# Two small multiplies per pass go from VectorE to GpSimd in a gated mix of two attentions

## The chip, the core and the metric

The kernel runs on one core of a Trainium2 chip. A core has five engines with their own instruction queues: TensorE (PE in the profile; PEld is its weight load), VectorE (DVE), ScalarE (ACT), GpSimd (POOL) and SyncE (SP), which here only issues DMAs. Each engine works through its queue in order, and the queues meet only at semaphores. The metric is the device time of one execution in microseconds; lower is better.

## The reference

The input x (2048 tokens, 512 wide) goes through two attention blocks of 32 heads of width 16, and a gate per token mixes the results:

```python
g = sigmoid((x * gate_w).sum(-1, keepdims=True))
a = A_ref(x, A_wq, A_wk, A_wv, A_wo, A_beta)
b = B_ref(x, B_wqkv, B_wo)
return g * a + (1 - g) * b
```

Block B is plain softmax attention over all 2048 keys. Block A cuts the tokens into four segments of 512, with causal softmax attention inside a segment and a linear memory M, z of the segments before it:

```python
p = softmax(q @ k.T * scale + mask); a_dot = p @ v
a_mem = (phi(q) @ M) / (phi(q) @ z + 1e-6)
o = sigmoid(beta) * a_mem + (1 - sigmoid(beta)) * a_dot
```

Both outputs go through an output projection. So for each head and token the kernel needs the softmax numerator, a denominator, and a factor for the numerator: g (1 - sigmoid(beta)) / denominator for A, (1 - g) / denominator for B.

## The kernel before, in words

The attention is cut into 64 units: 32 of A (u = 0 to 31) and 32 of B (u = 32 to 63). A unit is one group of four heads (qd) in one segment of 512 queries (c). The order of all instructions is written out by hand. After a first stage of projections, the main loop runs over k = 0 to 31; here one turn of it is called pass k. Pass k does B's unit 32 + k and A's unit k.

A pass is a sequence of steps n. In each of the first 32 steps PE computes a group of scores (`t_group`, L537) into PSUM, ACT turns an earlier group into exponentials (L543), and PE multiplies exponentials by V (`pv`, L559) into the bank pvb; V carries a column of ones, so row 16 of each head's result is the denominator. Woven between the matmuls of the step is one task of a *later* unit: `s_b` (L474) computes scores once more, two matmuls into one half of a double buffer (sbk), and DVE takes their row maximum with a reduce (L476), so that the exponentials can be shifted by it. There is one such reduce in each of the 32 steps, up to pass 30. Five more steps do A's unit: scores, exponentials, a triangular mask on POOL (`affine_select`, L546), and A's row maxima (`s_a`).

What the change touches is the end of a unit, spread over the next pass. `fin_copy` copies pvb out of PSUM and stores it (pd). `fin_load` loads back the numerators (o) and the denominators (rec, 128 partitions x 16). `fin_rec` (L580 on) takes the reciprocal on DVE, multiplies it by the gate, and stores it (rd, L589). `fin_bc` (L595) loads rd spread over the rows of a head (d), and `fin_norm` (L599, L604) multiplies numerators by d on POOL. In pass k the call `beside(k, it)` (it is half of n) runs `fin_rec` for B's unit 31 + k at it = 5 and for A's unit k - 1 at it = 6. `fin_norm` for two units at a time follows in the even passes, at it = 9 for B and 13 for A. `m_chain`, which prepares the row maxima of the next units, stands at it = 10; from pass 7 on it runs on POOL behind one small DVE reduce (L485, then L494 to L497). `m_rows` (it = 12) transposes its result on PE, and SP writes it into the q tiles (L515).

The gate columns were prepared long before: grow[:, 0] holds g, grow[:, 1] holds 1 - g, and nq holds 1 - sigmoid(beta), one column for each qd.

Of the kernel before, what the change touches and what calls it, by code (L numbers as in the profile page):

```python
# [12 lines left out]
OP = mybir.AluOpType  # L13
# [21 lines left out]
def gated_mix_kernel(ctx, tc, xt, wq, wk, wv, wo, beta, wqkv, wob, gate_w, out):  # L35
    nc = tc.nc
# [18 lines left out]
    grow = P.tile([128, 2, NC4, E], FT, name="grow")  # L55
    gh = P.tile([128, 4], FT, name="gh")
    nh = P.tile([128, 4], FT, name="nh")
    nq = P.tile([128, 8], FT, name="nq")
# [521 lines left out]
    def fin_rec(u):  # L580
        kd, qd, c = UN[u]
        r = AT.pop(("r", u))
        nc.vector.reciprocal(r, r)
        if kd == "A":
            nc.vector.scalar_tensor_tensor(r, r, nq[:, qd:qd + 1], grow[:, 0, c], op0=OP.mult, op1=OP.mult)
        else:
            nc.vector.tensor_tensor(r, r, grow[:, 1, c], op=OP.mult)
        AT["rd", u] = D.tile([128, E], FT, name=f"rd{u}")
        nc.sync.dma_start(AT["rd", u], r)  # L589

# [146 lines left out]
    early = st33[:EARLY]  # L737
# [21 lines left out]
    for blk in range(16):  # L759
        g, c = divmod(blk, 4)  # L760
# [135 lines left out]
    def beside(k, it):  # L896

        for f, it0, u in ((fin_load, NT + 1, 32 + k), (fin_rec, 5, 31 + k), (fin_bc, 6, 31 + k),
                          (fin_load, 1, k - 1), (fin_rec, 6, k - 1), (fin_bc, S_LAST + 2, k - 1)):
            if it == it0 and (k or it0 > NT):  # L900
                f(u)
        c, j = divmod(k - 1, 8)
        if k and j % 2:
            for kd, it0 in (("B", 9), ("A", 13)):
                if it == it0:
                    fin_norm(kd, j // 2, c)
        if k >= 8 and k % 2 == 0 and it == NT + 2:
            out_split(k // 8 - 1, k // 2 % 4)
        if (k, it) == (31, 4):
            grest = AT["grest"] = AT["o"][0][64:, 0, 0]  # L910
            nc.sync.dma_start(grest, GD[3 * C:].rearrange("(o t) -> o t", o=1).to_broadcast([64, C]))
        if (k, it) == (31, 9):
            grest = AT["grest"]
            nc.vector.tensor_scalar(grest, grest, nh[64:, 3:4], None, op0=OP.mult)
        if (k, it) == (31, NT + 2):
            fin_rec(63)
        if k == 31 and it == 13:
            o = AT["o"][1][:64, 3, 0]
            nc.gpsimd.tensor_tensor(o, o, AT["d"][0][:64], op=OP.mult)
        if k == 31 and it < 8 and it % 2 == 0:  # L920
            for a in range(2):
                tail_split(it // 2, slice(0, 3), a)
# [109 lines left out]
```

## Time and profile before

| | |
|---|---|
| median of 3 runs | 1946.82 us |
| lowest and highest | 1943.4 and 2188.65 us |
| profiled execution | 1946.74 us |
| its span in the trace | 1945.0 us |
| granted TensorE clock, mean | 0.997 |
| fin_rec's instructions on DVE | 63 reciprocals (L583), 31 for A (L585), 32 for B (L587) |

The span is the time from the first to the last instruction that the profiler recorded; 1.74 us of the profiled execution lie outside of it. In the rows of the profile a line such as `1000.17 0.24 DVE L583 RECIPROCAL rec<-rec` reads: start in us from the span's start, time in us, engine, line of the kernel, operation, output and input; `x8` at the end means that eight like instructions were merged into one row. A bracket tells how long the engine had been idle and what it had waited for.

### The profile page before, as it was taken

The numbers are of one execution on the slowest core, as the hardware profiler recorded it, in microseconds if no ns is written. First come the engines' busy times: TensorE is split into PE (matmuls) and PEld (weight loads), VectorE is DVE, ScalarE is ACT, GpSimd is POOL, SyncE is SP. The second block draws the span as 40 slices with busy tenths as digits, with TensorE's granted clock in tenths as the row PEclk, the third lists the DMA queues.
The fourth block names the chain that finished last, engine by engine and source line by source line (L and its number), as shares of the span: only waits on it lengthen the run. The fifth ranks groups of instructions, "written<-read, shape, count | busy, mean of one in ns | idle before, by whom it ended". The sixth has DMA issues, their size and how long they took to land.

```text
span 1945.0 us, 43560 instructions
## 1 busy us (share of the span) xinstructions
PE 1922.5 (99%) x17485; PEld 931.0 (48%) x17485; DVE 1622.1 (83%) x1726; ACT 1434.8 (74%) x2699; POOL 298.4 (15%) x593
## 2 busy tenths in 40 slices
PE   7999999999999999999999999999999999999999
PEld 5887777444344444444444444444444444444445
DVE  6135766899999999999999999999999999999942
ACT  4233333688888888888888888888888888888884
POOL 5200000011111111111111111111111111111022
PEclk9999999999999999999999999999999999999999
DMA  7666656745444444443445454544444443434111
GB/s 217 163 207 185 196 193 173 176 96 116 98 117 88 105 87 105 87 116 87 116 87 114 87 115 87 116 88 108 94 97 107 96 105 87 104 87 110 50 48 58
DMA packets 163790, 222.49 MB, mean 114 GB/s; under 512 B 39916, under 2 KB 90556, under 8 KB 157828
## 3 DMA queue, kind: packets, MB, share of 16 engines
q1 hardware_dynamic: 159284, 211.41, 44.1%
q0 software_dynamic: 3248, 8.03, 2.3%
q8 instruction: 138, 2.26, 0.5%
q14 instruction: 64, 0.52, 0.1%
q10 hardware_dynamic: 1056, 0.26, 0.1%
HBM read 147.95 MB, written 68.16 MB: 111 GB/s over the span
## 4 chain that ended last, share of the span: by engine, by line
PE 96%; DVE 2%; DMA 1%; SPq 1%; issue 0%; ACT 0%; DVEq 0%; ACTq 0%
PE pvb L559 33%; PE tb L537 18%; PE sbk L474 12%; PE mb L537 9%; PE tb L304 5%; PE sbk L452 3%; PE tb L625 2%; PE mb L304 2%; PE sbk L287 1%; PE tb L287 1%; PE mb L625 1%; PE pvb L304 1%; PE sbk L456 1%; PE mb L287 1%; PE pvb L287 1%; PE tb L652 1%
## 5 line engine op out<-in xcount | busy, mean ns | idle before, releaser
L476 DVE TENSOR_REDUCE mxb<-sbk 128x2 f32<-128x1024 f32 x1024 | 1225.8, 1223 | 61.0 <-PE tb L537 30.6
L543 ACT ACTIVATE raw<-tb 128x512 f32<-128x512 f32 x1555 | 887.6, 598 | 148.2 <-PE tb L537 103.6
L559 PE MATMUL pvb<-raw,vb 128*17 128x256 f32 (+1 forms) x8072 | 639.9, 388 | 0.0
L543 ACT ACTIVATE raw<-mb 128x512 f32<-128x512 f32 x782 | 467.6, 598 | 72.3 <-PE mb L537 45.7
L474 PE MATMUL sbk<-xh,qb 64*128 64x512 f32 x1344 | 477.6, 444 | 3.5 <-DVE mxb L476 2.1
L537 PE MATMUL tb<-qb,xh 64*128 64x512 f32 x872 | 353.3, 443 | 0.0
L559 PEld LDWEIGHTS pvb<-raw,vb 128*17 128x17 f32 x8072 | 135.0, 95 | 341.3 <-issue 335.9
L474 PE MATMUL sbk<-kb,qb 64*128 64x512 f32 x704 | 240.9, 444 | 0.0
L537 PEld LDWEIGHTS tb<-qb,xh 64*128 64x128 f32 x872 | 146.4, 184 | 176.6 <-issue 90.1
L537 PE MATMUL mb<-qb,xh 64*128 64x512 f32 x445 | 199.0, 447 | 0.0
L474 PEld LDWEIGHTS sbk<-xh,qb 64*128 64x128 f32 x1344 | 190.6, 184 | 8.7 <-DVE mxb L476 6.3
L537 PE MATMUL tb<-qb,kb 64*128 64x512 f32 x470 | 191.0, 446 | 0.9 <-DVE st L314 0.9
L546 POOL TENSOR_SCALAR_AFFINE_SELECT raw<-raw 128x256 f32<-128x256 f32 (+1 forms) x320 | 115.6, 361 | 357.7 <-ACT raw L543 349.9
L460 DVE TENSOR_REDUCE mx<-sbk 128x2 f32<-128x768 f32 (+1 forms) x128 | 136.7, 1090 | 23.7 <-PE sbk L456 20.9
L537 PEld LDWEIGHTS mb<-qb,xh 64*128 64x128 f32 x445 | 82.0, 184 | 94.9 <-issue 50.6
L537 PEld LDWEIGHTS tb<-qb,kb 64*128 64x128 f32 x470 | 79.2, 184 | 99.0 <-issue 53.1
L599 POOL TENSOR_TENSOR o<-o,d 128x512 f32<-128x512 f32 x31 | 39.7, 1280 | 477.7 <-DMA d<-rd 388.5
L537 PE MATMUL mb<-qb,kb 64*128 64x512 f32 x234 | 104.1, 445 | 0.0
L474 PEld LDWEIGHTS sbk<-kb,qb 64*128 64x128 f32 x704 | 96.1, 184 | 5.2 <-issue 3.4
L559 PE MATMUL pvb<-raw,va 128*17 128x256 f32 (+2 forms) x1280 | 94.7, 384 | 0.8 <-ACT pvs L568 0.8
L452 PE MATMUL sbk<-ka,qa 64*128 64x256 f32 (+3 forms) x512 | 88.0, 358 | 1.1
L311 ACT ACTIVATE st<-tb 128x512 fp32r<-128x512 f32 x33 | 19.8, 599 | 81.1 <-DVE phi L310 46.8
(288 smaller groups left out, 1864.3 us busy)
## 6 DMA issues: line engine op xcount, KB each, us to landing
xh<-dB SPq DMA_DIRECT2D x38, 512.0 KB
vb<-vdB SPq DMA_DIRECT2D x16, 1088.0 KB
dB<-st SPq DMA_DIRECT2D x64, 256.0 KB
dA<-st SPq DMA_DIRECT2D x64, 256.0 KB
pd<-pvs SPq DMA_DIRECT2D x64, 256.0 KB
kb<-dB SPq DMA_DIRECT2D x22, 512.0 KB
xh<-dB SPq DMA_DIRECT2D x38, 256.0 KB
qb<-dB SPq DMA_DIRECT2D x64, 128.0 KB
```

The costliest lines, as they stand in the source:

```text
L287: nc.tensor.matmul(b, lhs, WV[wi][:, k, :], start=n == 0, stop=n == 11)
L304: nc.tensor.matmul(b, WS[ws][w][wi][:, k, :], (XH, XL)[xi][c][:, k, :], start=n == 0, stop=n == 11)
L452: nc.tensor.matmul(b[:, j, c0:c0 + n], q_of(u)[r, p, i * 128:(i + 1) * 128], k_of(u, p)[r, :n], start=True, stop=False)
L460: nc.vector.tensor_reduce(m[:, :, p, i], b[:, :, :n], axis=AX.X, op=OP.max)
L474: nc.tensor.matmul(b[:, j], q_of(u)[r, p, i * 128:(i + 1) * 128], k_of(u, p)[r, kc * C:(kc + 1) * C], start=True, stop=True)
L476: nc.vector.tensor_reduce(MXB[u][:, :, p, i, kc], b, axis=AX.X, op=OP.max)
L537: nc.tensor.matmul(bs[j][:, c0:c0 + w], k_of(u, h // 2)[r, 128 * it:128 * it + 128], q_of(u)[r, h // 2, q0:], start=True, stop=True)
L543: nc.scalar.activation(pt, bs[j], AF.Exp, scale=SCALE)
L546: nc.gpsimd.affine_select(out=m, in_=m, pattern=[[1, 128]] if n < 2 else [[0, 2], [1, 128]], compare_op=OP.is_ge, fill=0.0, base=0, channe ...
L559: nc.tensor.matmul(PVB[32 * h:32 * h + E + 1, q0 + lo:q0 + hi], vt[:, it, 4 * q + h, :], pt[:, lo:hi], start=it == 0 and lo == 0, stop=it ...
L599: nc.gpsimd.tensor_tensor(o, o, d, op=OP.mult)
L625: nc.tensor.matmul(b, (AT["oh"], AT["ol"])[oi][:, g, a], (AT["wh"], AT["wl"])[wi][:, g, a], start=n == 0, stop=n == 11)
```

## The change

`early` is true for A's units 0 to 6 and 31 and for B's units 32 to 38 and 63. Those keep their form. For all others the multiply by the gate is issued on GpSimd. For A, one DVE instruction with two multiplications (by the column of nq, then by grow) becomes two POOL instructions; for B, one becomes one. Since the units 7 to 30 and 39 to 62 are finished in the passes 8 to 31, it is these 24 passes that change. The reciprocal stays on DVE, and the store of rd stays on SP.

```diff
         r = AT.pop(("r", u))
         nc.vector.reciprocal(r, r)
-        if kd == "A":
+        early = u % 32 < 7 or u in (31, 63)
+        if kd == "A" and not early:
+            nc.gpsimd.tensor_scalar(r, r, nq[:, qd:qd + 1], None, op0=OP.mult)
+            nc.gpsimd.tensor_tensor(r, r, grow[:, 0, c], op=OP.mult)
+        elif kd == "A":
             nc.vector.scalar_tensor_tensor(r, r, nq[:, qd:qd + 1], grow[:, 0, c], op0=OP.mult, op1=OP.mult)
         else:
-            nc.vector.tensor_tensor(r, r, grow[:, 1, c], op=OP.mult)
+            (nc.vector if early else nc.gpsimd).tensor_tensor(r, r, grow[:, 1, c], op=OP.mult)
         AT["rd", u] = D.tile([128, E], FT, name=f"rd{u}")
         nc.sync.dma_start(AT["rd", u], r)
```

On VectorE, in the first half of a pass, the queue before reads (rec is the tile with the 128 x 16 denominators, mxb the row maxima, sbk_114 and sbk_115 the two halves of the double buffer):

```order
L476 TENSOR_REDUCE mxb<-sbk_115 128x2
L583 RECIPROCAL rec<-rec 128x16
L587 TENSOR_TENSOR rec<-rec,grow 128x16
L476 TENSOR_REDUCE mxb<-sbk_114 128x2
L476 TENSOR_REDUCE mxb<-sbk_115 128x2
L583 RECIPROCAL rec<-rec 128x16
L585 SCALAR_TENSOR_TENSOR rec<-rec,nq,grow 128x16
L476 TENSOR_REDUCE mxb<-sbk_114 128x2
```

and at the same place of the changed kernel:

```order
L476 TENSOR_REDUCE mxb<-sbk_115 128x2
L583 RECIPROCAL rec<-rec 128x16
L476 TENSOR_REDUCE mxb<-sbk_114 128x2
L476 TENSOR_REDUCE mxb<-sbk_115 128x2
L583 RECIPROCAL rec<-rec 128x16
L476 TENSOR_REDUCE mxb<-sbk_114 128x2
```

The two multiplies are gone; the reduces and reciprocals keep their order.

On GpSimd, the changed kernel's queue from the masks of one pass to those of the next reads as follows (the new rows are L591 for B and L586 and L587 for A; L603 is the line that was L599 before the change; the brackets name the semaphores that an instruction waits for):

```order
L546 AFFINE_SELECT raw_86<-raw_86 128x2x128 [waits Activation_49] x6
L591 TENSOR_TENSOR rec<-rec,grow 128x16 [waits DMAHW4_49,DVE_49]
L586 TENSOR_SCALAR rec<-rec,nq 128x16 [waits DMAHW6_49,DVE_49]
L587 TENSOR_TENSOR rec<-rec,grow 128x16 [waits Pool_49]
L603 TENSOR_TENSOR o_2775<-o_2775,d_2779 128x512 [waits DMAHW7_49,DMAHW6_49,DMAHW5_49]
L494 TENSOR_SCALAR mx<-mx 128x32 [waits DVE_49]
L495 CAST mhi<-mx 128x32 [waits Pool_49]
```

The three new instructions stand between the masks and `fin_norm`; what came before stays in its order.

On SyncE, the stores of the gates in the first half of a pass read before

```order
L589 DMA rd_13448<-rec 128x16 [waits DMAHW4_49,DVE_49]
L595 DMA d_2779<-rd_13448 64x1x512 [waits DMAHW5_49,DMAHW4_49]
L589 DMA rd_13475<-rec 128x16 [waits DMAHW6_49,DVE_49]
L394 DMA qa_74<-dA_118 32x2x512 [waits DMAHW7_49,PE_49]
L394 DMA qa_74<-dA_118 32x2x512 [waits PE_49]
```

and now

```order
L593 DMA rd_13460<-rec 128x16 [waits DMAHW4_49,Pool_49]
L599 DMA d_2779<-rd_13460 64x1x512 [waits DMAHW5_49,DMAHW4_49]
L593 DMA rd_13488<-rec 128x16 [waits DMAHW6_49,Pool_49]
L394 DMA qa_74<-dA_118 32x2x512 [waits DMAHW7_49,PE_49]
L394 DMA qa_74<-dA_118 32x2x512 [waits PE_49]
```

Only the wait differs: the stores wait for POOL where they waited for DVE.

## The prediction

> **What bounds the kernel now.** I read the page first, then the stages, then the chain that ended last, and last the rows around one place that the change touches. The page's first part and its chain:
>
> ```profile
> PE 1922.5 (99%) x17485; PEld 931.0 (48%) x17485; DVE 1622.1 (83%) x1726; ACT 1434.8 (74%) x2699; POOL 298.4 (15%) x593
> PE 96%; DVE 2%; DMA 1%; SPq 1%; issue 0%; ACT 0%; DVEq 0%; ACTq 0%
> ```
>
> TensorE (PE) is the bound: it is never free for long, and the chain runs along it. That doesn't yet say that the other engines cost nothing, because a matmul that waits for a PSUM bank hides inside a busy neighbour. A stretch from the middle shows how near VectorE (DVE) stands to it (columns: stretch, length, then busy time and instructions of PE, weight loads, DVE, ACT, POOL, then granted clock, DMA share, GB/s):
>
> ```profile
> core 0: us, PE busy (x) PEld busy (x) DVE busy (x) ACT busy (x) POOL busy (x), PEclk, DMA share, GB/s
> 1000.00:1200.00 200.00, 199.86 (x2036) 84.09 (x2036) 186.12 (x182) 167.08 (x311) 30.58 (x64) 1.00 0.44 99
> ```
>
> There DVE is busy 186 of 200 us, at a granted clock of 1.00, and POOL 31. So PE sets the pace with DVE close behind, and a DVE instruction costs time only where it makes a PSUM bank come free too late. Such places can be seen in the rhythm of the chain. One step of a pass ends in eight rows of the PV product (L559), and a step's length is the distance between two of these (three excerpts of the chain: pass 9, pass 13, pass 30):
>
> ```profile
> 804.41 0.56 PE pvb L559 x8
> 805.62 0.56 PE pvb L559 x8
> 807.00 0.56 PE pvb L559 x8
> ...
> 1002.65 0.56 PE pvb L559 x8
> 1003.86 0.56 PE pvb L559 x8
> 1005.24 0.56 PE pvb L559 x8
> ...
> 1846.56 0.56 PE pvb L559 x8
> 1847.92 0.56 PE pvb L559 x8
> ```
>
> A step takes 1.21 to 1.22 us (804.41 to 805.62, 1002.65 to 1003.86). One step takes 1.38, 1.38 and 1.36 in these three passes: 0.16, 0.16 and 0.14 us too long. Here is why, at the middle one:
>
> ```profile
> 1003.14 0.18 PEld L537 LDWEIGHTS tb<-qb,xh 64*128 64x128 f32 x1 [0.42 <-issue]
> 1003.14 0.29 PEld L474 LDWEIGHTS sbk<-xh,qb 64*128 64x128 f32 x2
> 1003.24 4.61 DVE L476 TENSOR_REDUCE mxb<-sbk 128x2 f32<-128x1024 f32 x4
> 1004.36 0.18 PEld L537 LDWEIGHTS tb<-qb,xh 64*128 64x128 f32 x1 [0.42 <-ACT raw L543]
> 1004.51 0.19 PEld L474 LDWEIGHTS sbk<-xh,qb 64*128 64x128 f32 x2
> ```
>
> In an ordinary step the score matmuls for the maxima (L474) load their weights together with the step's first product (L537): both at 1003.14. In the long step they come at 1004.51 instead of 1004.36. They need the bank that the first of the four reduces is still reading: it starts at 1003.24, and one reduce takes 1.22, so it ends at 1004.46.
>
> **What the change takes from VectorE.** The reduces before that one were late because of the two gate steps. DVE in order of time in pass 13, and the same eight reduces of pass 14:
>
> ```profile
> 997.81 2.44 DVE L476 TENSOR_REDUCE mxb<-sbk 128x2 f32<-128x1024 f32 x2
> 1000.17 0.24 DVE L583 RECIPROCAL rec<-rec 128x16 f32<-128x16 f32 x1
> 1000.45 0.18 DVE L587 TENSOR_TENSOR rec<-rec,grow 128x16 f32<-128x16 f32 x1
> 1000.54 2.35 DVE L476 TENSOR_REDUCE mxb<-sbk 128x2 f32<-128x1024 f32 x2
> 1002.80 0.24 DVE L583 RECIPROCAL rec<-rec 128x16 f32<-128x16 f32 x1
> 1003.08 0.24 DVE L585 SCALAR_TENSOR_TENSOR rec<-rec,nq,grow 128x16 f32<-128x16 f32 x1
> 1003.24 9.36 DVE L476 TENSOR_REDUCE mxb<-sbk 128x2 f32<-128x1024 f32 x8
> 1012.51 0.21 DVE L485 TENSOR_REDUCE mx<-mxb 128x16 f32<-128x64 f32 x1
> 1012.63 3.62 DVE L476 TENSOR_REDUCE mxb<-sbk 128x2 f32<-128x1024 f32 x3
> ...
> 1052.80 9.36 DVE L476 TENSOR_REDUCE mxb<-sbk 128x2 f32<-128x1024 f32 x8
> ```
>
> Undisturbed, DVE starts a reduce every (9.36 - 1.22) / 7 = 1.16 us, a little faster than PE's 1.22, so it catches up by 0.06 us a step and no more. Around the B pair, the last reduce starts at 997.81 + 2.44 - 1.22 = 999.03 and the next at 1000.54: 1.51, that is 0.35 more than a plain step. Around the A pair it is 1003.24 - (1000.54 + 2.35 - 1.22) = 1.57, 0.41 more. Together 0.76 us within three steps; the double buffer hides all but about 0.15 of it.
>
> After the change each place keeps only the reciprocal. How soon a reduce follows a lone reciprocal isn't in the trace. The nearest rows bound it: after the small reduce L485 the next one starts 0.12 later (1012.51 to 1012.63), and the dependent multiply starts 0.28 after its reciprocal (1000.17 to 1000.45). I take 0.15, near the first, because reduce and reciprocal don't depend on each other. A reduce is followed by the reciprocal after 1000.17 - 999.03 = 1.14, so the distance becomes 1.29 at either place. DVE gets back 1.51 - 1.29 = 0.22 and 1.57 - 1.29 = 0.28, together 0.50 us per pass. With 0.28 in place of 0.15 it is 0.09 + 0.15 = 0.24. Both are more than the 0.15 that PE loses. What is late next: with 0.50 the bank is free at 1003.96, 0.40 before PE asks for it at 1004.36; with 0.24 at 1004.22, still 0.14 ahead. So the long step becomes an ordinary one, and the rest of the freed DVE time (24 x (0.175 + 0.235) = 9.8 us in all, from the two groups below) falls into DVE's idle time.
>
> ```profile
> L585 DVE SCALAR_TENSOR_TENSOR rec<-rec,nq,grow 128x16 f32<-128x16 f32 x31 | 7.3, 235 | 1.1
> L587 DVE TENSOR_TENSOR rec<-rec,grow 128x16 f32<-128x16 f32 x32 | 5.6, 175 | 1.1
> ```
>
> **Passes that count.** The multiplies move in passes 8 to 31. Pass 31 has no maxima left to compute, so nothing waits there. In pass 8 the corresponding step isn't long:
>
> ```profile
> 756.12 0.56 PE pvb L559 x8
> 757.36 0.56 PE pvb L559 x8
> ```
>
> That is 1.24. There remain passes 9 to 30, 22 of them, at 0.15: **3.3 us**.
>
> **What it adds.** POOL gets one multiply for B and two for A in each pass: 72 instructions. The trace has none of 128x16 on POOL; the nearest are
>
> ```profile
> L494 POOL TENSOR_SCALAR mx<-mx 128x32 f32<-128x32 f32 x24 | 6.9, 289 | 381.8 <-DVE mx L485 381.8
> L497 POOL TENSOR_TENSOR m<-mx,mhi 128x32 f32<-128x32 f32 x24 | 6.0, 251 | 0.0
> ...
> 1012.81 0.29 POOL L494 TENSOR_SCALAR mx<-mx 128x32 f32<-128x32 f32 x1 [27.01 <-DVE mx L485]
> 1055.77 1.28 POOL L599 TENSOR_TENSOR o<-o,d 128x512 f32<-128x512 f32 x1 [23.36 <-DMA d<-rd]
> ```
>
> I take 0.22 for a two-input multiply and 0.29 for the multiply by a column of nq (bounds: nothing, and L599's 1.28). POOL stands idle there: for 27 us before 1012.81, for 23 us before 1055.77. In its queue behind the new work come fin_norm's multiply (L599), which waits for a DMA anyway, and m_chain (L494), which waits for DVE anyway. The new wait that counts is SP's: the store of the gates (L589) now waits for POOL, and SP's loads stand behind it.
>
> ```profile
> 1000.65 0.34 SPq L589 DMA_DIRECT2D rd<-rec  x1
> 1002.12 0.52 SPq L595 DMA_DIRECT2D d<-rd  x1
> 1003.35 0.33 SPq L589 DMA_DIRECT2D rd<-rec  x1
> ...
> 1007.17 0.43 SPq L420 DMA_DIRECT2D va<-vdA  x1
> 1016.12 1.14 SPq L515 DMA_DIRECT2D qb<-mr  x2
> ```
>
> B: the reciprocal ends at 1000.41, POOL starts 0.09 later (as L494 behind L485: 1012.72 to 1012.81), takes 0.22, and the store goes out at about 1000.74 instead of 1000.65. A: about 0.2 later than 1003.35, since its reciprocal comes 0.22 sooner. The loads behind it end near 1007.8 instead of 1007.6, and SP then has nothing to do until 1016.12. This costs nothing; the cover is those 8.5 us.
>
> **The sum.** The profiled execution took 1946.74 us (span 1945.0 and 1.74 around it), practically the median of 1946.82. 1946.74 - 3.3 = **1943.4 us**, 0.17% faster. A measurement of this kernel can tell about 2% (39 us) from no change, so this counts as no change.
>
> **Rivals.** (1) *DVE sets the pace*, and all of its freed time comes out: 24 x 0.41 = 9.8 us, 1936.9. For it: 186 of 200 us busy. Against it: only one step in a pass is long for that reason. (2) *The stall stays*, because a lone reciprocal holds the next reduce as long as the pair did, or because another unit is late by as much: 1946.7. (3) *Slower: POOL's multiplies hold DVE up.* If DVE stood still while POOL works, a pass would lose 0.22 + 0.29 + 0.22 = 0.73 and get back 0.50; the long step would grow by 0.23, in 23 passes 5.3 us: 1952.0. It begins to eat the gain when DVE loses more than 0.50 - 0.15 = 0.35 per pass, and turns slower above 0.50. Against it stand two rows above: the eight reduces from 1003.24 on, with POOL idle, take 9.36, and those from 1052.80 on, with L599's 1.28 us among them, take 9.36 too. The Trainium skill, page "SBUF — State Buffer", section "SBUF: two separate sides", says that GpSimd and VectorE share one pair of ports under an exclusive lock, but that VectorE takes it only in a two-port mode or with two SBUF inputs. By that rule the reduces, which read PSUM, aren't held, and the trace agrees: 9.36 and 9.36. A lock on every instruction would give the 1952.0. (4) *SP held by POOL*: if the two A multiplies took more than 8.5 us, the loads would push the row maxima's transfers and the pass; 2% needs 1.6 us a pass beyond that. At 0.29 for the nearest instruction this is remote. (5) *The change does less than it says*, some multiplies staying on DVE: the instruction order shows them moved, so this has no share of its own.
>
> **Chances.** Forecast 0.77, rival 1 0.06, rival 2 0.09, rival 3 0.06, rival 4 and the like 0.02. The two lower times before differ by 3.4 us (1943.4 and 1946.8), so each value carries about that: the forecast spans 1940 to 1947, rival 2 reaches 1948.5, and the low end goes to 1938 for a partial rival 1. Range 1938 to 1948.5. Faster by over 2% 0.01, within 2% 0.97, slower by over 2% 0.02.
>
> **What would show it.** In the profile after: the L559 row behind the A reciprocal 1.22 after the one before it; L474's weights loaded together with L537's; reduces 1.29 apart around a reciprocal; each of passes 9 to 30 shorter by 0.15; POOL's new instructions at 0.2 to 0.3, idle before them; SP's stores 0.1 to 0.2 later and its loads still done long before the row maxima's. The prediction is wrong if the step stays at 1.36 or grows, if reduces beside POOL's multiplies are longer than 1.22, or if another step of the pass becomes longer.

## The result and the profile after

The changed kernel takes 1942.13 us (median of 22 runs, 1936.84 to 1945.18); the kernel before, timed beside it, 1946.02 us (median of 22). The ratio is 0.9984, with a 95% interval of 0.9978 to 0.9990: faster by 0.16%, far inside the 2% that count as no change, and clear of zero. The ratio comes from all executions but one slow one of the kernel before (2188.65 us), and the interval stands for 1.9 to 4.3 us; the two medians alone lie 3.9 us apart. The prediction was 1943.4 us, 0.17% faster. The profiled execution after took 1943.65 us with a span of 1941.9 us, 3.1 us less than the 1945.0 before. Whole times vary by several us from one execution to the next, so that 0.16 and 0.17% lie so close is in part luck; the firmer check is the same stretch of instructions in both traces, below.

First the engines' busy times over the whole, from the page of the profile after:

```profile
PE 1918.9 (99%) x17485; PEld 927.4 (48%) x17485; DVE 1619.4 (83%) x1678; ACT 1434.8 (74%) x2699; POOL 317.4 (16%) x665
```

DVE has 48 instructions less and POOL 72 more. DVE's busy time falls by only 2.7 us although 9.8 us of multiplies left it. Busy time counts a moment once, also where two instructions overlap. The eight reduces behind A's step of pass 13 took 9.36 us in all before, each starting before the one ahead of it had ended; now they come when PE is ready for them and take 9.67 us in all. The place to look at is again the rhythm of the chain (the step behind A's reciprocal in passes 9, 13 and 30 of the kernel after):

```profile
805.60 0.56 PE pvb L559 x8
806.83 0.56 PE pvb L559 x8
...
1003.49 0.56 PE pvb L559 x8
1004.72 0.56 PE pvb L559 x8
...
1843.55 0.56 PE pvb L559 x8
1844.77 0.56 PE pvb L559 x8
```

These are the steps that took 1.36 to 1.38 us; they now take 1.22 to 1.23. The same holds in each of the passes 9 to 30: by the starts of the L559 rows in the two traces, the step took 1.34 to 1.38 us before and takes 1.22 after. The weight loads of that step and VectorE and GpSimd around it (pass 13, in order of time):

```profile
1002.24 0.24 DVE L583 RECIPROCAL rec<-rec 128x16 f32<-128x16 f32 x1
1002.40 4.80 DVE L476 TENSOR_REDUCE mxb<-sbk 128x2 f32<-128x1024 f32 x4
1002.58 0.33 POOL L586 TENSOR_SCALAR rec<-rec,nq 128x16 f32<-128x16 f32 x1 [2.23 <-DVE rec L583]
...
1003.99 0.18 PEld L537 LDWEIGHTS tb<-qb,xh 64*128 64x128 f32 x1 [0.42 <-ACT raw L543]
1003.99 0.29 PEld L474 LDWEIGHTS sbk<-xh,qb 64*128 64x128 f32 x2
```

The reduce follows the lone reciprocal by 0.16 us, and L474 loads its weights together with L537 again. The stretch from the B reciprocal of pass 9 to that of pass 31 sums it up: the two executions over the same instructions (first the kernel before, then after; columns as in the prediction).

```profile
801.90:1882.70 1080.80, 1080.00 (x10966) 454.97 (x10964) 992.87 (x968) 903.73 (x1682) 168.23 (x352) 1.00 0.42 96
```

```profile
801.90:1879.50 1077.60, 1076.57 (x10966) 451.62 (x10964) 991.02 (x924) 903.67 (x1682) 185.55 (x418) 1.00 0.42 96
```

The same 10,966 matmuls take 1077.6 us in place of 1080.8: 3.2 us over the 22 passes 9 to 30, 0.145 each on average. The 22 long steps alone add up to 29.99 us before and 26.83 after, also 3.2 less, so the whole difference lies in this one step of a pass. What follows the stretch is equally long to 0.1 us. That both stretches begin at 801.90 is chance: after the change the first B reciprocal came 0.18 us later, and passes 1 to 8 together were 0.19 us shorter (pass 3 by 0.27, pass 8 by 0.10, while pass 6 was 0.18 longer).

### The profile page after: what moved, and what is told of

It is laid out like the page before. It is cut to its first block, busy times and chain, and to the rows that moved or that the text cites. A ratio compares the mean times of both kernels' runs of the same rounds, so it can differ in the third digit from the quotient of the medians.

```text
span 1941.9 us, 43661 instructions
## 1 busy us (share of the span) xinstructions
PE 1918.9 (99%) x17485; PEld 927.4 (48%) x17485; DVE 1619.4 (83%) x1678; ACT 1434.8 (74%) x2699; POOL 317.4 (16%) x665
## 4 chain that ended last, share of the span: by engine, by line
PE 96%; DVE 2%; DMA 0%; ACT 0%; SPq 0%; issue 0%; DVEq 0%; ACTq 0%
PE pvb L559 33%; PE tb L537 18%; PE sbk L474 12%; PE mb L537 9%; PE tb L304 5%; PE sbk L452 3%; PE tb L629 2%; PE mb L304 2%; PE sbk L287 1%; PE tb L287 1%; PE pvb L304 1%; PE mb L629 1%; PE sbk L456 1%; PE mb L287 1%; PE pvb L287 1%; DVE mxb L476 1%
## 5 line engine op out<-in xcount | busy, mean ns | idle before, releaser
L559 PE MATMUL pvb<-raw,vb 128*17 128x256 f32 (+1 forms) x8072 | 639.9, 388 | 0.0
L474 PE MATMUL sbk<-xh,qb 64*128 64x512 f32 x1344 | 479.8, 445 | 3.8 <-DVE mxb L476 1.8
L537 PE MATMUL tb<-qb,xh 64*128 64x512 f32 x872 | 352.2, 443 | 0.0
L559 PEld LDWEIGHTS pvb<-raw,vb 128*17 128x17 f32 x8072 | 134.9, 95 | 341.3 <-issue 335.9
L474 PE MATMUL sbk<-kb,qb 64*128 64x512 f32 x704 | 242.1, 444 | 0.0
L537 PEld LDWEIGHTS tb<-qb,xh 64*128 64x128 f32 x872 | 145.9, 185 | 176.6 <-issue 89.7
L537 PE MATMUL mb<-qb,xh 64*128 64x512 f32 x445 | 198.9, 447 | 0.0
L474 PEld LDWEIGHTS sbk<-xh,qb 64*128 64x128 f32 x1344 | 192.2, 184 | 9.1 <-DVE mxb L476 6.1
L537 PE MATMUL tb<-qb,kb 64*128 64x512 f32 x470 | 191.1, 447 | 0.8 <-DVE st L314 0.8
L537 PEld LDWEIGHTS mb<-qb,xh 64*128 64x128 f32 x445 | 82.1, 184 | 94.9 <-issue 50.4
L537 PEld LDWEIGHTS tb<-qb,kb 64*128 64x128 f32 x470 | 79.2, 184 | 98.8 <-issue 53.1
L537 PE MATMUL mb<-qb,kb 64*128 64x512 f32 x234 | 104.0, 444 | 0.0
L474 PEld LDWEIGHTS sbk<-kb,qb 64*128 64x128 f32 x704 | 96.8, 184 | 5.2 <-issue 3.5
L559 PE MATMUL pvb<-raw,va 128*17 128x256 f32 (+2 forms) x1280 | 94.7, 384 | 0.8 <-ACT pvs L568 0.8
L311 ACT ACTIVATE st<-tb 128x512 fp32r<-128x512 f32 x33 | 19.8, 598 | 81.4 <-DVE phi L310 47.3
L537 PE MATMUL tb<-qa,ka 64*128 64x512 f32 (+3 forms) x339 | 79.5, 372 | 0.0
```

The source lines that it names most:

```text
L311: nc.scalar.activation(st[:, 0], b, AF.Copy)
L474: nc.tensor.matmul(b[:, j], q_of(u)[r, p, i * 128:(i + 1) * 128], k_of(u, p)[r, kc * C:(kc + 1) * C], start=True, stop=True)
L537: nc.tensor.matmul(bs[j][:, c0:c0 + w], k_of(u, h // 2)[r, 128 * it:128 * it + 128], q_of(u)[r, h // 2, q0:], start=True, stop=True)
L559: nc.tensor.matmul(PVB[32 * h:32 * h + E + 1, q0 + lo:q0 + hi], vt[:, it, 4 * q + h, :], pt[:, lo:hi], start=it == 0 and lo == 0, stop=it ...
```

## The experiments

The prediction held, so the question is whether it held for its reason: a backlog on DVE that outgrows the double buffer at one step of a pass, and not DVE's total of work. Each run was timed beside the kernel before, its ratio is to that kernel, and below, "the stretch" is the time from the B reciprocal of pass 9 to that of pass 31, 1080.8 us in the kernel before. Each run has one profile.

### One half of the change at a time

Both edits are made to the changed kernel. The first leaves B's multiply on DVE:

```diff
-            (nc.vector if early else nc.gpsimd).tensor_tensor(r, r, grow[:, 1, c], op=OP.mult)
+            nc.vector.tensor_tensor(r, r, grow[:, 1, c], op=OP.mult)
```

> Only A's multiplies go to POOL; B's stay on DVE. Theory (a stall of 0.15 us per pass, gone as soon as DVE gets back more than that before the A step): A alone frees 0.27 us, so the long step of passes 9 to 30 becomes 1.22 and the whole 3.3 us come: ratio to before 0.9983, the same as the full change. Rival (every DVE us counts): 24 x 0.235 = 5.6 us. Rival (the gain is shared in proportion): about 0.56 of the gain, 1.8 us, long step near 1.28.

The second leaves A's multiplies on DVE:

```diff
-        if kd == "A" and not early:
+        if False:
```

> Only B's multiply goes to POOL; A's stays on DVE. Theory: B alone frees 0.21 us before the A step, still more than 0.15, so the long step becomes 1.22, or at most 1.24, and 2.9 to 3.3 us come. Rival (every DVE us counts): 24 x 0.175 = 4.2 us. Rival (shared in proportion): 0.44 of the gain, 1.5 us, long step near 1.30.

With A alone moved the kernel took 1941.62 us, ratio 0.9976 (0.9966 to 0.9986), and the stretch 1077.6. With B alone it took 1943.98 us, ratio 0.9983 (0.9974 to 0.9992), and the stretch 1078.0. Each half gains what the whole gains (1077.6), to within 0.4 us. VectorE and the chain with only B's multiply moved (pass 13):

```profile
1004.28 0.24 DVE L583 RECIPROCAL rec<-rec 128x16 f32<-128x16 f32 x1
1004.56 0.23 DVE L589 SCALAR_TENSOR_TENSOR rec<-rec,nq,grow 128x16 f32<-128x16 f32 x1
1004.71 8.19 DVE L476 TENSOR_REDUCE mxb<-sbk 128x2 f32<-128x1024 f32 x7
...
1005.54 0.56 PE pvb L559 x8
1006.76 0.56 PE pvb L559 x8
```

A's slow pair is still there (0.43 from the start of the reciprocal to that of the reduce), and yet the step behind it is 1.22 long. With A alone or B alone, the step is 1.22 in each of the passes 9 to 30; the 0.4 us that B alone has over 1077.6 lie elsewhere, most of it in passes 18 and 26. So a gain in proportion to the freed time is ruled out, and so is DVE's sum as the bound: half the freed time buys all of the gain at this step.

### All of the work, at another place

```diff
-                          (fin_load, 1, k - 1), (fin_rec, 6, k - 1), (fin_bc, S_LAST + 2, k - 1)):
+                          (fin_load, 1, k - 1), (fin_rec, 9, k - 1), (fin_bc, S_LAST + 2, k - 1)):
```

This is the kernel before with A's `fin_rec` three turns of `it` later; no instruction leaves DVE.

> All multiplies stay on DVE as before, but the A step is done at it = 9 instead of 6, so that DVE has six more steps to catch up at 0.06 us a step. Theory (backlog): 0.41 for A meets a DVE that has recovered about 0.35 of B's delay; no step is long any more in passes 1 to 30, 29 x 0.147 = 4.3 us below before, ratio 0.9978, with not a single DVE instruction less. Rival (DVE's sum of time counts, or the multiply as such costs): no gain, the long step only moves to it = 9.

It took 1940.91 us, ratio 0.9972 (0.9962 to 0.9982), and the stretch 1077.4: the same gain in passes 9 to 30 as the change, with all 63 multiplies still on DVE. This shows that it was the meeting of two delays within three steps, not the multiplies' sum. VectorE around the two places and the chain at the second, pass 13 (both steps there are ordinary):

```profile
997.05 0.24 DVE L583 RECIPROCAL rec<-rec 128x16 f32<-128x16 f32 x1
997.32 0.18 DVE L587 TENSOR_TENSOR rec<-rec,grow 128x16 f32<-128x16 f32 x1
997.41 9.46 DVE L476 TENSOR_REDUCE mxb<-sbk 128x2 f32<-128x1024 f32 x8
1006.80 0.24 DVE L583 RECIPROCAL rec<-rec 128x16 f32<-128x16 f32 x1
1007.07 0.23 DVE L585 SCALAR_TENSOR_TENSOR rec<-rec,nq,grow 128x16 f32<-128x16 f32 x1
...
1008.05 0.56 PE pvb L559 x8
1009.27 0.56 PE pvb L559 x8
```

One part of the expectation missed. In passes 1 to 6 `m_chain` still runs on DVE, at it = 10, and now stands close behind A's pair: there the step at `m_rows` takes 1.66 instead of 1.40 us (430.79 to 432.45 in the chain of pass 1, against 432.44 to 433.84 before), and passes 1, 2, 4, 5 and 6 are 0.1 us longer instead of 0.15 shorter. The stall had only moved, to the next place where two delays meet. So the ratio, which is lower than the 0.9978 expected, can't be due to these passes. In its profile, whose span of 1939.2 us is 5.8 less than before, 3.3 us come from the stretch, 1.5 from an earlier start of the main loop, and 1.3 from pass 3 (47.6 us in place of 48.8), which escaped a delay that the section on the hardware tells of. The first is the effect, the second chance; whether the later `fin_rec` makes the third more likely, one profile can't tell. The start alone varies by more than the miss: the first B reciprocal came at 415.1 to 419.6 us in the ten profiles.

### The change in all passes

This is the changed kernel with the multiplies on POOL from pass 1 on.

```diff
-        early = u % 32 < 7 or u in (31, 63)
+        early = u in (31, 63)
```

> The change in all passes 1 to 31. Theory: the long step of passes 1 to 7 (1.36 before and after the change) becomes 1.22 too: 7 x 0.145 = 1.0 us more than the change, 4.3 us below before, ratio 0.9978; nothing is lost to the copies of the output weights on POOL in passes 1 to 4, because they stand later in the pass. Rival: in passes 1 to 4 POOL is still held by the weights when the multiplies come, and the gain there is lost or turned round.

It took 1940.88 us, ratio 0.9972 (0.9962 to 0.9981). The long step is 1.22 in passes 1 to 5 and 7 too, and passes 1, 2, 4 and 5 take 47.3 us each in place of 47.45 to 47.49. In pass 6 it is 1.32, since A's reciprocal waited 0.39 us there for the load of its denominators. Four of the ten profiles have such a wait of 0.3 to 0.6 us in one or two of the passes 6 to 8, with a step of 1.32 to 2.07 us behind it, two of them in pass 7 of kernels that differ from the one before only from pass 8 on. So this wait isn't tied to the change. The lead of this run over the change, expected as 1 us, is smaller than what the intervals can tell (0.9962 to 0.9981 against 0.9978 to 0.9990). In its profile one pass, the third, was 1.5 us longer than in the kernel before, for a reason that the section on the hardware tells; so this run doesn't show 1 us either, only that the step is ordinary in the early passes too.

### More work on VectorE

To the kernel before, a useless small multiply is added behind each of the two gate multiplies.

```diff
             nc.vector.tensor_tensor(r, r, grow[:, 1, c], op=OP.mult)
+        if u not in (31, 63):
+            nc.vector.tensor_tensor(W.tile([128, E], FT, name="dum"), r, grow[:, 1, c], op=OP.mult)
```

> The kernel before, with one more small VectorE multiply (128x16, into a tile that nobody reads) behind each of the two gate multiplies. Theory: the double buffer's slack is used up before the A step, so here every further bit of DVE time comes out in full: a dependent small multiply delays the next reduce by about 0.21 at either place, 0.41 per pass, in 30 passes 12.3 us, long step near 1.77, ratio 1.006. If the slack were not used up, some of the 0.41 would not be seen; if a multiply counted only by its own 0.175, it would be 0.35 per pass and 10.5 us.

It took 1956.78 us, ratio 1.0057 (1.0044 to 1.0071), and the span was 1956.9, 11.9 us more than before. The chain of pass 13:

```profile
1006.23 0.56 PE pvb L559 x8
1007.54 0.56 PE pvb L559 x8
1008.76 0.56 PE pvb L559 x8
1010.44 0.56 PE pvb L559 x8
```

Now two steps are long: 1.31 (B's delay alone already outgrows the buffer) and 1.68, where one of 1.77 was expected. As means over passes 9 to 30 they are 1.31 and 1.69 in place of 1.22 and 1.36, together 0.09 + 0.32 = 0.41 us more, and the stretch (1090.0 us) is 9.2 longer, 0.42 per pass: the loss has the size that was worked out, but falls on two steps. So the price of the same small DVE instruction depends on the side of the threshold: all of it above; below, as the half changes show, nothing.

### POOL kept busy

To the changed kernel, useless multiplies of 128x512 are added behind B's multiply on POOL in passes 8 to 31, first four (`...` stands for the lines that set up their tiles):

```diff
             (nc.vector if early else nc.gpsimd).tensor_tensor(r, r, grow[:, 1, c], op=OP.mult)
+            if not early:
+                ...
+                for _ in range(4):
+                    nc.gpsimd.tensor_tensor(AT["dum"], w0, w1, op=OP.mult)
```

> The changed kernel, with four useless POOL multiplies of 128x512 (about 1.28 us each) behind B's multiply in passes 8 to 31, so that POOL is busy for 5.2 us beside some four reduces and beside the A reciprocal, and A's multiplies and SP's store of A's gates come about 3 us later. Theory: reduces read PSUM and aren't held, and SP has 8.5 us to spare: no step becomes longer, within 0.2% of the changed kernel, ratio to before 0.9983. One place is open: the reciprocal works in SBUF; if POOL holds it too, the step behind it can grow by up to 1 us less the 0.40 of slack. Rival (POOL holds every DVE instruction): about 5 us a pass, over 100 us in all.

It took 1942.58 us, ratio 0.9983 (0.9973 to 0.9992), and the stretch 1077.9. POOL and VectorE of pass 13:

```profile
997.12 5.38 POOL L597 TENSOR_TENSOR dum<-wh,wl 128x512 f32<-128x512 f32 x4
1002.48 0.33 POOL L586 TENSOR_SCALAR rec<-rec,nq 128x16 f32<-128x16 f32 x1
...
996.78 2.37 DVE L476 TENSOR_REDUCE mxb<-sbk 128x2 f32<-128x1024 f32 x2
999.07 0.24 DVE L583 RECIPROCAL rec<-rec 128x16 f32<-128x16 f32 x1
999.23 9.70 DVE L476 TENSOR_REDUCE mxb<-sbk 128x2 f32<-128x1024 f32 x8
```

POOL works from 997.1 to 1002.5 without a break. The reduces beside it and the reciprocal take as long as in the changed kernel (9.70 us for eight reduces against 9.67 there, 0.24 for the reciprocal), and A's multiplies come 3.1 us later than there without harm. The question that the expectation left open is answered: the reciprocal isn't held. In this trace 22 reciprocals lie wholly within one of the useless multiplies, and each took 0.24 us. With twelve in place of four:

> As the run before, but with twelve useless POOL multiplies: POOL is held for 15.4 us a pass. Theory: this is beyond the cover. SP's store of A's gates comes near 16 us after the B reciprocal, its loads behind it late; m_chain on POOL comes late for m_rows on PE, by about 2.5 us in the odd and 3.8 in the even passes; 23 passes by 3.1 give some 72 us, about 2014 us, ratio 1.037. If SP's loads were what is waited for, the stall would be seen before the masks at the end of the pass instead of at m_rows.

It took 2071.56 us, ratio 1.0672 (1.0632 to 1.0711), where 1.037 was expected. The place was right and the size too small: from pass 10 to pass 28 the odd passes are 3.4 us longer than with the change, the even ones about 7.0. The chain in pass 10:

```profile
877.28 1.22 POOL o L609
878.50 0.27 POOL mx L494
...
879.10 0.22 POOL m L496
879.37 0.85 PE tb L507 x4
881.37 0.98 PE pvb L559 x8
883.50 0.98 PE pvb L559 x8
```

PE waits at L507 (the transposes of `m_rows`) for `m_chain`, which is queued on POOL behind the useless work and `fin_norm` (L609); SP's late loads are not what is waited for. Two terms were missing. Multiplies in a row start 1.36 us apart and not 1.28 (the twelve take 16.24 us in pass 13), which is 0.8 us a pass. And after the longer wait PE runs slowly for a while: the two steps behind it take 2.13 us each. The stretches of that pass show why (columns as in the prediction):

```profile
874.00:879.00 5.00, 1.18 (x12) 0.31 (x12) 1.87 (x2) 1.43 (x3) 4.73 (x7) 1.00 0.07 11
879.20:885.90 6.70, 6.53 (x36) 2.31 (x40) 2.68 (x3) 3.03 (x7) 0.33 (x2) 0.50 0.89 252
```

The granted clock is 0.50 over the 6.7 us behind the idle stretch. So a wait of PE of this length (4.2 us) is paid for twice.

### VectorE multiplies beside a busy POOL

This is the kernel before, multiplies on DVE, with POOL kept busy by four useless multiplies as above. The small POOL multiply ahead of them reads B's result, so that POOL's useless work begins only behind it (`...` again stands for lines of set-up; `early` here spares passes 1 to 7).

```diff
             nc.vector.tensor_tensor(r, r, grow[:, 1, c], op=OP.mult)
+            ...
+            if not early:
+                ...
+                nc.gpsimd.tensor_tensor(AT["dum"][:, :E], r, r, op=OP.mult)
+                for _ in range(4):
+                    nc.gpsimd.tensor_tensor(AT["dum"], w0, w1, op=OP.mult)
```

> The kernel before (both gate multiplies on VectorE), with the four useless POOL multiplies of 128x512 and one small one ahead of them behind B's multiply in passes 8 to 31, so that POOL is at work when A's reciprocal and A's multiply (two SBUF inputs) come on VectorE. In the trace of before, pass 3, a VectorE instruction with two SBUF inputs (L501) lasted 1.28 us instead of 0.31 while POOL worked on a 128x512 multiply. Theory (a lock between POOL and such VectorE instructions): A's multiply (L585) lasts not 0.235 but 0.3 to 1.3 us in these passes, and the long step grows by 0.3 to 1.7 us, 7 to 39 us in all, ratio 1.004 to 1.02. Rival (no lock): L585 stays at 0.235, the long step at 1.36, ratio 1.000.

It took 1953.50 us, ratio 1.0041 (1.0027 to 1.0056), and the stretch 1088.7, 7.9 us longer. VectorE, POOL and the chain of pass 13:

```profile
1001.41 0.58 DVE L585 SCALAR_TENSOR_TENSOR rec<-rec,nq,grow 128x16 f32<-128x16 f32 x1
...
999.32 5.35 POOL L595 TENSOR_TENSOR dum<-wh,wl 128x512 f32<-128x512 f32 x4
...
1002.19 0.56 PE pvb L559 x8
1003.91 0.56 PE pvb L559 x8
```

A's multiply takes 0.58 us in place of 0.235. It ends at 1001.99, just behind the end of the second of POOL's four multiplies. The same holds in each of the passes 9 to 30: L585 takes 0.58 to 0.60 us and ends 0.03 us after that multiply. The step grows to 1.72, by the same 0.35. (The expectation gave 0.31 as the ordinary time of L501; that was a mean with the one long instance in it, and the ordinary value is 0.185.)

## Why the prediction was right, point by point

**The bound.** PE sets the pace at 1.22 us a step, and DVE matters only where its delay makes a PSUM bank come free too late. This was right: moving the delays apart gave the gain without taking anything from DVE.

**What VectorE gets back.** A distance of 1.29 between the reduces around a lone reciprocal was estimated; the trace after shows 1.30 (the reduce ahead of the B reciprocal starts at 998.66, the next at 999.96; around the A one they start at 1001.10 and 1002.40). So 0.48 came back for the 0.50 forecast. The bank is free at 1002.40 + 1.22 = 1003.62, which is 0.37 before PE asks for it at 1003.99; 0.40 was forecast. That more than 0.15 is enough, and the rest worth nothing, is shown by the two half changes.

**Passes that count.** The 22 passes were right; pass 31 gained nothing, and pass 8 at most 0.03 us at this step. They gained 0.145 us each in place of 0.15, together 3.2 us in place of 3.3.

**What it adds.** The groups of POOL in the kernel after:

```profile
L586 POOL TENSOR_SCALAR rec<-rec,nq 128x16 f32<-128x16 f32 x24 | 7.9, 328 | 51.8 <-DVE rec L583 51.8
L587 POOL TENSOR_TENSOR rec<-rec,grow 128x16 f32<-128x16 f32 x24 | 5.5, 228 | 2.0
L591 POOL TENSOR_TENSOR rec<-rec,grow 128x16 f32<-128x16 f32 x24 | 5.4, 224 | 376.9 <-DVE rec L583 376.9
```

The two-input multiplies were taken as 0.22 and took 0.22 to 0.23; the multiply by a column of nq was taken as 0.29 and takes 0.33. POOL was idle before them. SP in pass 13:

```profile
1000.37 0.34 SPq L593 DMA_DIRECT2D rd<-rec  x1
...
1003.24 0.33 SPq L593 DMA_DIRECT2D rd<-rec  x1
...
1007.07 0.43 SPq L420 DMA_DIRECT2D va<-vdA  x1
1015.59 1.14 SPq L515 DMA_DIRECT2D qb<-mr  x2
```

Counted from the start of B's reciprocal (999.80) the stores go out after 0.57 and 3.44 us instead of 0.48 and 3.18, so 0.09 and 0.26 later (0.09 and 0.2 forecast), and SP then still has 8.1 us to spare. Four useless multiplies showed that a store of A's gates 3 us late costs nothing; what twelve cost came from POOL's queue and not from SP.

**The rivals.** DVE's total as the pace was ruled out by the half changes, and the stall that stays by the trace after. POOL holding DVE up did not happen in this kernel. The prediction named the condition under which it would, two SBUF inputs, but not that the multiplies themselves meet it: on DVE they could be held by a busy POOL; on POOL they meet only reduces and reciprocals there, which aren't held. In the kernel before POOL stood idle beside them (no L585 took more than 0.236 us and no L587 more than 0.177), so an end to such holds is no part of the gain. The rival of a POOL queue that is too long has its place at `m_rows`, through `m_chain`, and not at SP's loads as the prediction had it.

## What to carry to other kernels

In a pipeline like this one, where a second engine runs a few per cent faster than the one that sets the pace, the cost of a small instruction on the second isn't its duration: it is nothing as long as the double buffer between them absorbs it, and all of it once the buffer is spent. Look in the chain for the one step that is longer than its neighbours and add up the delays just ahead of it; taking away the excess, or moving two delays apart, is worth as much as removing all of the work. Before work goes to another engine's queue, ask which later instruction of that queue the bound engine waits for, and how long the queue may be held until then.

## What the runs showed of the hardware that was not expected

**POOL can hold VectorE.** The two queues meet at more than semaphores. It was already in the trace of the kernel before, in pass 3, VectorE above (L499 to L501 are `m_chain` in its form for VectorE) and POOL below (L611 and L612 split weights of the output projection into two parts):

```profile
526.34 0.45 DVE L499 TENSOR_SCALAR mhi<-mx 128x32 fp32r<-128x32 f32 x1
526.83 0.18 DVE L500 COPY m<-mhi 128x32 f32<-128x32 f32 x1
526.92 1.28 DVE L501 SCALAR_TENSOR_TENSOR m<-mx,mhi 128x32 f32<-128x32 f32 x1
...
526.15 0.61 POOL L611 CAST wh<-o 128x512 fp32r<-128x512 f32 x1 [27.43 <-DMA o<-in_A_wo_dram]
526.84 1.31 POOL L612 TENSOR_TENSOR wl<-o,wh 128x512 fp32r<-128x512 f32 x1
```

L499 and L501 ordinarily take 0.18 us each. Here L499 ends with POOL's cast (526.79 and 526.76) and L501 with POOL's subtraction (528.20 and 528.15). Together with the run that kept POOL busy beside A's multiply this shows: an instruction of VectorE with two SBUF inputs (L501, L585) ended only when POOL's running instruction had ended, and so did the one-input L499 between two SBUF tiles, while a reduce from PSUM (1.22 us) and the 128x16 reciprocal (0.24 us) kept their times beside a busy POOL. The Trainium skill, page "SBUF — State Buffer", section "SBUF: two separate sides", states this lock for VectorE instructions with two SBUF inputs or in a two-port mode; the runs agree (0.58 for 0.235, 1.28 for 0.185). Whether L499 runs in such a mode no run here shows. The meeting depends on when the DMA lands that POOL's cast waits for, and it makes pass 3 longer in some executions than in others: in the ten profiles it took 47.5 to 47.9 us in the three where neither L499 nor L501 was held, and 48.6 to 50.4 us in the seven where one or both were. (The 50.4 belong to the run with the change in all passes; there PE's wait of 1.2 us was also followed by 3.4 us at half clock, from 528.1 us on.) In the run with B alone both were held in pass 1 too, which took 48.8 us.

**A long wait of PE costs twice.** In the run with twelve useless multiplies, PE stood still from about 875.2 to 879.4 us, and its granted clock was then 0.50 over 6.7 us. In that run PE waited 4.2 us at L507 in each even pass from 10 to 28, each time with 6.8 us at half clock from about the end of the wait on; in the odd passes 11 to 27 it waited 3.0 us, and the clock stayed at 1.00. The Trainium skill, page "TensorE: Matmul & The Clock Gate", section "What's actually happening", says that the clock falls to half after an idle window of about 3.4 us; the even and odd passes agree. An estimate by that page alone, one window at half speed (1.7 us lost) or two (3.4), encloses what the even passes lost beyond the longer wait (7.0 - 3.4 - 1.3 for `fin_norm` = 2.3 us). But the 3.4 us are no sharp limit here: the clock also fell for 3.4 us behind waits of 3.0 us in passes 9 and 29 of this run, and behind the 1.2 us in pass 3 of the run with the change in all passes. Why it fell there stays open.
